# One row maximum over two score banks instead of two maxima

## The chip, the cores and the metric

The kernel runs on one core of a Trainium2 chip. The metric is the device time of one launch in microseconds (us); the time before is the median of three runs. One further execution was recorded by the hardware profiler, and all rows below come from it. Engines are named as in the profile: PE (matrix multiplications), PEld (its weight loads), DVE (vector engine), ACT (scalar engine), POOL (GpSimd), SP (the queue that issues DMAs). PSUM, where matmuls write, has eight banks of 512 fp32 numbers per partition.

## What is computed

An attention with a learned decay, and then a mixture of four experts on its output. Cut to what matters:

```python
# q, k, v: (4, 8, 576, 64); s: (4, 8, 576)
scores = scale * np.matmul(q, k.transpose(0, 1, 3, 2))
cum = np.cumsum(np.maximum(s, 0.0), axis=-1)
bias = -(cum[:, :, :, None] - cum[:, :, None, :])
scores = np.where(causal, -1000000000.0, scores + np.minimum(bias, 0.0))
scores = scores - np.max(scores, axis=-1, keepdims=True)
attn = np.exp(scores)
attn = attn / (np.sum(attn, axis=-1, keepdims=True) + 1e-09)
x = np.matmul(attn, v)        # then reshaped to (2304, 512)
for e in range(4):            # experts, 512 -> 1024 -> 512
    out += p[:, e:e + 1] * (np.maximum(x @ w1[e], 0.0) @ w2[e])
```

## The kernel before

There are 32 heads (`BH`). The 576 rows of a head are cut into five query tiles, m = 0 to 4; because of the causal mask tile m needs only its first 64, 192, 320, 448 or 576 scores. The list `VISITS` says which tiles of which head are done together: the first eight heads come twice (tiles 0 to 2, later tiles 3 and 4), the other 24 once with all five. So tile 4, the last, occurs 32 times.

For each tile the chain is: scores on PE into a bank `S` (line 584 for the first heads, one fp32 matmul; line 587 for the others, two matmuls for each piece), row maximum on DVE (line 597, a fused instruction that adds the mask, scales, writes the scores to SBUF tile `a` and keeps the maximum in `mx`, followed by a short instruction that reads the accumulator), exponential and row sum on ACT (line 605), 1/sum (lines 611, 613), the normalisation (line 402, mostly POOL), transposes on PE into a bank `T` (line 635), copies out of it by ACT (407) and DVE (671), and the product with v on PE into `pv` (694).

PSUM holds two `S` banks, two `T` banks, two for `pv` and two `mo` banks for the expert. Tile 4 has 576 scores and does not fit one bank, so it is made in two pieces of 288, each in one `S` bank: matmuls and a maximum for each piece, the second maximum starting from the first one's result:

```python
pieces = [(0, bb)] if bb <= 512 else [(0, 288), (288, bb)]
```

The order of all engines' instructions in this part is written out before the kernel is built, by a list scheduler (`Sched`). A task names its engines with an assumed cost, its priority, and the buffers that it takes and gives back. Each engine takes the ready task of the best priority whose buffers are free. `S` tiles may also borrow an `mo` bank (`sources`). While attention runs, PE's gaps are filled with matmuls of the first expert (lines 786 and 799) at a lower priority, and early on with matmuls that only keep PE busy (line 426). What is left of the first expert, and the other three (lines 1087, 1097), follow after the last attention task. PE takes its instructions strictly in the order that results, and so do the others. The waits between engines are put in when the program is built: an instruction waits on another engine's counter until the last accesses of a buffer that it reuses are done.

Of the kernel before, what the change touches and what calls it, by code (L numbers as in the profile page):

```python
# [139 lines left out]
class Task:  # L140
    def __init__(self, engs, fn, deps, prio, take, give, xfer):
        self.engs = {e: c if isinstance(c, tuple) else (c, 0) for e, c in engs.items()}
        self.fn, self.prio, self.take, self.give, self.xfer = fn, prio, take, give, xfer
        self.wait = 0
        self.ready = 0.0
        self.next = []
        self.after = []
        self.done = None
        self.eng = None
        self.act = 0.9  # L150
        self.port = ()
        self.both = False


class Sched:
# [30 lines left out]
        return t  # L186

    def sources(self, t, p, lend):
        if p in ("S", "T") and lend:
            return (p, "mo")  # L190
        if t.prio < 1000.0 * NH + 900:
            return LEND.get(p, (p,))
        return (p,)

    def run(self, until):
# [22 lines left out]
        while left:  # L218
            moved = False
            lend = not any(t.prio >= 1e6 and t.ready <= now + LAHEAD for t in cand["PE"])  # L220
            nxt = []
            for e in names:
                if free[e] > now:
                    nxt.append(free[e])
                    continue
                best = None
                for t in cand[e]:
                    if best is not None and t.key > best.key:
                        continue
                    if t.ready + t.engs[e][1] > now:  # L230
                        nxt.append(t.ready + t.engs[e][1])
                        continue
                    if t.xfer is not None and self.dma_free > now + BACKLOG:
                        nxt.append(self.dma_free - BACKLOG)
                        continue
                    if e in t.port and self.port > now:
                        nxt.append(self.port)
                        continue
                    ok = True
                    for p, k in t.take:  # L240
                        f = min((b[0] for x in self.sources(t, p, lend) for b in self.pools[x]), default=1e18)
                        if f > now:
                            ok = False
                            if f < 1e17:
                                nxt.append(f)
                            break
                    if ok:
                        best = t
                if best is None:
                    if e == "PE" and self.warm and active() < FILL:  # L250
                        x = dummy(now)
                        if x:
                            free[e] = now + x
                            nxt.append(free[e])
                            moved = True
                    elif e == "PE" and self.warm:
                        nxt.append(now + 100)
                    continue
                t = best
                extra = 0  # L260
                if e == "PE" and now > T_HAM:
                    self.warm = None
                if e == "PE" and self.warm and t.prio < 1e6 and active() < KEEP:
                    extra = dummy(now)
                moved = True
                for x in t.engs:
                    cand[x].remove(t)
                for p, k in t.take:
                    x, b = min(((x, b) for x in self.sources(t, p, lend) for b in self.pools[x]), key=lambda y: y[1][0])
                    self.pools[x] = [y for y in self.pools[x] if y is not b]  # L270
                    self.tok[p, k] = b[1]
                    self.home[p, k] = x
                t.fn(e)
                end = now + extra + t.engs[e][0]
                if e == "PE":
                    acts.append((now + extra, end, t.act))
                free[e] = end
                if e in t.port:
                    self.port = end
                if t.xfer is not None:  # L280
                    self.dma_free = max(self.dma_free, end + 700) + t.xfer / RATE
                    end = self.dma_free + 900
                t.done, t.eng = end, e
                left.discard(id(t))
                for p, k in t.give:
                    self.pools[self.home.pop((p, k))].append([end + 150, self.tok.pop((p, k))])
                for n in t.after:
                    n.wait -= 1
                    if n.wait == 0:
                        for x in n.engs:  # L290
                            cand[x].append(n)
                for n in t.next:
                    n.wait -= 1
                    n.ready = max(n.ready, end + (LAG[e][0] if e in n.engs else LAG[e][1]))
                    if n.wait == 0:
                        for x in n.engs:
                            cand[x].append(n)
                nxt.append(free[e])
            if not moved:
                later = [x for x in nxt if x > now]  # L300
                assert later, "schedule stuck"
                now = min(later)


def body(ctx, tc, qk, vp, s, dp, w1, w1s, w2, w2s, out):
# [10 lines left out]
    def make(name, n, shape, dt=F32, pool=apool):  # L316
        sch.pool(name, [pool.tile(shape, dt, name=f"{name}_{i}") for i in range(n)])
# [21 lines left out]
    def AB(j, dt=F32R):  # L339
        return slot(tok["AB", j], [P, 2, S], dt, apool)  # L340

    pattn = actx.enter_context(tc.tile_pool(name="psa", bufs=1, space=PSUM))
    make("S", 2, [P, 512], pool=pattn)
    make("T", 2, [P, 512], pool=pattn)
    make("pv", 1, [P, 1024], pool=pattn)
    make("mo", 2, [P, 512], pool=psum)
# [152 lines left out]
    for j, (h, ms) in enumerate(VISITS):  # L499
# [36 lines left out]
        else:  # L536
            if pq:
                qk_ready = [ld, ldc]
            else:
# [7 lines left out]
                def f(e, j=j, h=h, ext=ext):  # L547
                    nc.sync.dma_start(out=tok["KK", j][0:64, :, 0:ext].bitcast(F32), in_=AB(j)[64:128, 0:1, 0:ext].bitcast(F32).to_broadcast([64, 2, ext]))
                    nc.sync.dma_start(out=tok["KK", j][64:128, 0, 0:ext].bitcast(F32), in_=AB(j)[64:128, 1, 0:ext].bitcast(F32))
                    nc.sync.dma_start(out=tok["KK", j][64:68, 1, 0:ext].bitcast(F32), in_=ced[h, 2:6, 0:ext])  # L550
# [17 lines left out]
        for m in ms:  # L568
# [2 lines left out]
            n = bb - a  # L571
            c = (j, m)

            pieces = [(0, bb)] if bb <= 512 else [(0, 288), (288, bb)]
            prev = None
            for pi, (j0, j1) in enumerate(pieces):
                lastp = pi == len(pieces) - 1

                def f(e, j=j, a=a, j0=j0, j1=j1, c=c, pi=pi, ext=ext, pq=pq, h=h):
                    t = tok["S", (c, pi)]  # L580
                    if pq:
                        r = AB(j, F32)
                        w = min(P, ext - a)
                        nc.tensor.matmul(t[0:w, 0:j1 - j0], r[0:66, 0, a:a + w], r[0:66, 1, j0:j1], start=True, stop=True)  # L584
                    else:
                        for x, k in ((0, P), (1, 68)):
                            nc.tensor.matmul(t[:, 0:j1 - j0], AB(j)[0:k, x, a:a + P], tok["KK", j][0:k, x, j0:j1], start=(x == 0), stop=(x == 1))  # L587
                qt = sch.add({"PE": (t_pe4(j1 - j0) if pq else 2 * t_pe(j1 - j0))}, f, qk_ready + [last_q], prio=pr + pi, take=[("S", (c, pi))],
                             give=([("AB", j)] if pq else [("AB", j), ("KK", j)]) if lastp and m == ms[-1] else [])
                last_q = qt  # L590
                qt.act = 0.5 if pq else 0.9
                firstq.setdefault(j, qt)

                def f(e, m=m, n=n, a=a, j0=j0, j1=j1, c=c, pi=pi):
                    mx = tok["mx", c]
                    z = tok[f"a{m}", c]
                    nc.vector.tensor_tensor_reduce(  # L597
                        out=z[0:n, j0:j1], in0=tok["S", (c, pi)][0:n, 0:j1 - j0], in1=mask[0:n, 448 - a + j0:448 - a + j1], scale=-0.125,
                        scalar=1e30 if pi == 0 else mx[0:n, 0:1], op0=ALU.add, op1=ALU.min, accum_out=mx[0:n, pi:pi + 1])
                prev = sch.add({"DVE": t_dve(j1 - j0)}, f, [qt, prev], prio=pr + pi,  # L600
                               take=[("mx", c), (f"a{m}", c)] if pi == 0 else [], give=[("S", (c, pi))])

            def f(e, m=m, n=n, bb=bb, c=c, k=len(pieces) - 1):
                z = tok[f"a{m}", c]
# [685 lines left out]
```

## Time and profile before

| what | value |
|---|---|
| median of three runs | 942.4 us (941.18, 942.4, 942.45) |
| the profiled execution, its own time | 941.22 us |
| span of its instructions | 939.3 us |
| PE busy over the span | 926.9 us (99%) |
| DVE busy | 714.4 us (76%) |
| PE clock granted, mean | 0.999 of full speed |

The span runs from the first to the last instruction; 1.9 us of the execution's time lie around it. Attention with the first expert's matmuls between takes up about the first 300 us. A matmul counts as busy while it is in flight, and those in flight overlap, so PE can be shown busy while its next instruction waits a short time.

### The profile page before, as it was taken

To read this page: it belongs to the slowest core of one execution; us is meant where nothing else is said; L and a number is where in the kernel's file an instruction comes from. 1 tells how busy PE (TensorE), PEld (TensorE's weight loads), DVE (VectorE), ACT (ScalarE), POOL (GpSimd) and SP (SyncE) were. 2 spreads that over 40 slices of the span, in tenths; PEclk is the share of its full clock that TensorE was granted. 3 is DMA by queue.
4 is the path that set the end of the run, shared out by engine and by line. 5 is a ranking of instruction groups with operands and counts; after the bars stand their busy time and mean duration, and the time that the engine had idled before them with its cause. 6 is when DMAs were issued, how large, how long until landed. Compare 5 with 4: busy or idle time off the path is not lost.

```text
span 939.3 us, 18269 instructions
## 1 busy us (share of the span) xinstructions
PE 926.9 (99%) x6304; PEld 881.9 (94%) x6304; DVE 714.4 (76%) x1803; ACT 454.6 (48%) x1167; POOL 456.5 (49%) x504
## 2 busy tenths in 40 slices
PE   9999999999999999999999999999999999999998
PEld 7778998898998998999999999999999999999998
DVE  7898887888886221368679977988797879678976
ACT  6788796777875110252444333434252524343340
POOL 5566574555641789312653173435343714471222
PEclk9999999999999999999999999999999999999999
DMA  5887677687642895487765558654785458744613
GB/s 154 235 220 217 179 202 213 169 214 209 168 123 99 272 386 194 168 299 261 235 230 177 195 195 281 201 185 155 256 276 182 140 202 278 235 153 150 220 33 118
DMA packets 125899, 189.73 MB, mean 202 GB/s; under 512 B 10432, under 2 KB 102112, under 8 KB 125808
## 3 DMA queue, kind: packets, MB, share of 16 engines
q1 hardware_dynamic: 125808, 188.57, 63.6%
q8 instruction: 50, 0.82, 0.4%
q14 instruction: 41, 0.34, 0.1%
HBM read 144.73 MB, written 29.54 MB: 186 GB/s over the span
## 4 chain that ended last, share of the span: by engine, by line
PE 89%; DVE 4%; issue 2%; ACT 2%; POOL 1%; DMA 1%; DVEq 0%; SPq 0%; ACTq 0%; POOLq 0%
PE pb L1087 26%; PE pb L1097 20%; PE mo L1097 8%; PE mo L799 7%; PE mo L786 6%; PE T L635 5%; PE pv L694 5%; PE S L587 4%; PE pb L786 3%; PE pb L799 3%; PE S L584 2%; DVE aTl L671 1%; DVE a L597 1%; ACT a L605 1%; DMA AB_f<-cx 1%
## 5 line engine op out<-in xcount | busy, mean ns | idle before, releaser
L1087 PE MATMUL pb<-x,w1h 128*128 128x384 f32 x1008 | 256.7, 335 | 0.5 <-ACT t L1127 0.3
L1087 PEld LDWEIGHTS pb<-x,w1h 128*128 128x128 f32 x1008 | 180.8, 188 | 2.5 <-DVE t L1131 1.8
L1087 PE MATMUL pb<-x,w1l 128*128 128x384 f32 x504 | 168.5, 334 | 0.0
L394 POOL TENSOR_TENSOR hT_r<-t,hT_r 128x768 fp32r<-128x768 f32 x18 | 34.0, 1887 | 268.6 <-PE pb L1087 215.6
L1127 ACT ACTIVATE t<-pb 128x384 f32<-128x384 f32 x144 | 66.4, 486 | 160.8 <-PE pb L1087 151.6
L1190 DVE SCALAR_TENSOR_TENSOR acc<-pb,prob,acc 128x256 f32<-128x256 f32 x288 | 125.8, 473 | 5.3 <-PE pb L1097 4.9
L1097 PE MATMUL pb<-w2h,hT_r 128*128 128x256 f32 x720 | 114.6, 283 | 0.1
L402 POOL TENSOR_SCALAR a<-a,sm 128x192 f32<-128x192 f32 (+4 forms) x142 | 79.9, 569 | 50.2 <-DVE sm L613 36.4
L1097 PEld LDWEIGHTS pb<-w2h,hT_r 128*128 128x128 f32 x720 | 99.6, 191 | 0.3 <-issue 0.3
L605 ACT ACTIVATE a<-a,mx 64x64 f32<-64x64 f32 (+4 forms) x160 | 89.3, 561 | 21.5 <-DVE mx L597 18.8
L1131 DVE TENSOR_TENSOR t<-pb,t 128x384 f32<-128x384 f32 x108 | 54.4, 549 | 57.6 <-PE pb L1087 36.1
L1087 PEld LDWEIGHTS pb<-x,w1l 128*128 128x128 f32 x504 | 94.6, 188 | 0.0
L1104 ACT ACTIVATE hT_r<-t 128x768 fp32r<-128x768 f32 x54 | 45.7, 846 | 98.2 <-PE pb L1097 92.7
L1101 DVE SCALAR_TENSOR_TENSOR t<-t 128x768 f32<-128x768 f32 x72 | 88.0, 1223 | 1.7 <-issue 1.6
L786 PE MATMUL mo<-xg,w1h 128*128 128x256 f32 (+1 forms) x360 | 83.6, 309 | 0.9 <-DVE hT_r L792 0.9
L407 ACT ACTIVATE aTh<-T 128x64 fp32r<-128x64 f32 (+2 forms) x278 | 66.3, 307 | 22.3 <-PE T L635 19.3
L635 PE MATMUL T<-idn,a 128*128 128x128 f32 x465 | 73.1, 276 | 3.5 <-DVE aTl L671 3.2
L671 DVE TENSOR_TENSOR aTl<-T,aTh 128x64 fp32r<-128x64 f32 (+3 forms) x246 | 72.6, 334 | 4.5 <-ACT aTh L407 3.3
L1097 PE MATMUL pb<-w2l,hT_r 128*128 128x256 f32 x360 | 71.5, 283 | 0.0
L597 DVE CUSTOM_DVE_ANT_0 a<-S,mask 128x320 f32<-128x320 f32 (+4 forms) x151 | 61.7, 420 | 8.9 <-PE S L584 4.2
L635 PEld LDWEIGHTS T<-idn,a 128*128 128x128 f32 x465 | 53.2, 141 | 15.4 <-issue 6.5
L1190 DVE SCALAR_TENSOR_TENSOR acc<-mo,prob,acc 128x256 f32<-128x256 f32 x144 | 62.7, 472 | 1.6 <-PE mo L1097 1.6
(149 smaller groups left out, 2086.8 us busy)
## 6 DMA issues: line engine op xcount, KB each, us to landing
x<-xs_d SPq DMA_DIRECT2D x68, 768.0 KB
x<-x_d SPq DMA_DIRECT2D x55, 768.0 KB
xs_d<-x SPq DMA_DIRECT2D x12, 768.0 KB
raw<-in_qk_dram SPq DMA_DIRECT2D x24, 288.0 KB
KK<-AB_r SPq DMA_DIRECT2D x24, 288.0 KB
x_d<-xh SPq DMA_DIRECT2D x12, 576.0 KB
w1r<-in_w1s_dram SPq DMA_DIRECT2D x6, 1024.0 KB
w2r<-in_w2s_dram SPq DMA_DIRECT2D x6, 1024.0 KB
```

The costliest lines, as they stand in the source:

```text
L402: (nc.gpsimd if e == "POOL" else nc.vector).tensor_scalar(out, in_, scale, 1.0 if bias is None else bias, op0=ALU.mult, op1=ALU.mult if bi ...
L597: nc.vector.tensor_tensor_reduce(out=z[0:n, j0:j1], in0=tok["S", (c, pi)][0:n, 0:j1 - j0], in1=mask[0:n, 448 - a + j0:448 - a + j1], scale ...
L605: nc.scalar.activation(z[0:n, 0:bb], z[0:n, 0:bb], AF.Exp, bias=tok["mx", c][0:n, k:k + 1], scale=-1.0, accum_out=tok["sm", c][0:n])
L635: nc.tensor.transpose(t[:, 128 * k:128 * k + 128], z[:, 128 * x:128 * x + 128], idn)
L671: nc.vector.tensor_tensor(out=dst, in0=src, in1=h_.bitcast(F32), op=ALU.subtract)
L786: nc.tensor.matmul(t[:, 0:w], wl[q][:, dc, o:o + P], xgt[:, l, dc, 0:w], start=(u == 0), stop=(u == 3 * KD - 1))
L799: nc.tensor.matmul(t, ht[:, fc, 128 * ti:128 * ti + 128], wl[fc // 2][:, fc % 2, :], start=(u == 0), stop=(u == 3 * KF - 1))
L1087: nc.tensor.matmul(ts[u][:, 0:TG], wv[wl][:, k, 128 * u:128 * u + 128], x[:, xl_, k, :], start=start and k == 0 and n == 0, stop=k == 1 an ...
L1097: nc.tensor.matmul(ts[t][:, 0:256], h_part(o, hl_)[:, k, 128 * t:128 * t + 128], wv[wl][:, k, :], start=start and k == 0 and n == 0, stop= ...
L1101: (nc.gpsimd if e == "POOL" else nc.vector).scalar_tensor_tensor(out=out, in0=in0, scalar=0.0, in1=in1, op0=ALU.max, op1=op)
L1127: nc.scalar.activation(tmp[name][:, u], ts[u][:, 0:TG], f)
L1190: nc.vector.scalar_tensor_tensor(out=a_, in0=ts[t][:, 0:256], scalar=prob[:, tt, e:e + 1], in1=a_, op0=ALU.mult, op1=ALU.add)
```

## The change

The two `S` banks become one PSUM tile of 1024 columns, `both`, and the two pool entries are its halves. Tiles 0 to 3 take one half as before. Tile 4 takes both halves at once (`whole`): its four matmuls write columns 224 to 511 and 512 to 799, which are neighbours across the bank border, and one row-maximum instruction reads all 576. A task that is `whole` can start only when both halves are free, and it may not borrow an `mo` bank. The planner's cost of the maximum becomes that of 576 columns, and the four matmuls are one task.

```diff
     def sources(self, t, p, lend):
-        if p in ("S", "T") and lend:
+        if p in ("S", "T") and lend and not t.whole:
             return (p, "mo")
...
                         f = min((b[0] for x in self.sources(t, p, lend) for b in self.pools[x]), default=1e18)
+                        if t.whole and p == "S":
+                            f = max(b[0] for b in self.pools[p]) if len(self.pools[p]) == 2 else 1e18
...
-    make("S", 2, [P, 512], pool=pattn)
+    both = pattn.tile([P, 1024], F32, name="S")
+    sch.pool("S", [both[:, 0:512], both[:, 512:1024]])
...
-            pieces = [(0, bb)] if bb <= 512 else [(0, 288), (288, bb)]
+            pieces = [(0, bb)]
+            halves = [(0, bb)] if bb <= 512 else [(0, 288), (288, bb)]
...
-                    t = tok["S", (c, pi)]
+                    for j0, j1 in halves:
+                        t = (tok["S", (c, pi)] if len(halves) == 1 else both[:, 224:800])[:, j0:j1]
...
-                            nc.tensor.matmul(t[:, 0:j1 - j0], AB(j)[0:k, x, a:a + P], tok["KK", j][0:k, x, j0:j1], start=(x == 0), stop=(x == 1))
+                                nc.tensor.matmul(t, AB(j)[0:k, x, a:a + P], tok["KK", j][0:k, x, j0:j1], start=(x == 0), stop=(x == 1))
-                qt = sch.add({"PE": (t_pe4(j1 - j0) if pq else 2 * t_pe(j1 - j0))}, f, qk_ready + [last_q], prio=pr + pi, take=[("S", (c, pi))],
+                whole = len(halves) > 1
+                held_s = [("S", (c, x)) for x in range(len(halves))]
+                qt = sch.add({"PE": sum(t_pe4(y - x) if pq else 2 * t_pe(y - x) for x, y in halves)}, f, qk_ready + [last_q], prio=pr + pi, take=held_s,
...
+                    t = both[:, 224:800] if whole else tok["S", (c, pi)]
...
-                        out=z[0:n, j0:j1], in0=tok["S", (c, pi)][0:n, 0:j1 - j0], in1=mask[0:n, 448 - a + j0:448 - a + j1], scale=-0.125,
+                        out=z[0:n, j0:j1], in0=t[0:n, 0:j1 - j0], in1=mask[0:n, 448 - a + j0:448 - a + j1], scale=-0.125,
...
-                               take=[("mx", c), (f"a{m}", c)] if pi == 0 else [], give=[("S", (c, pi))])
+                               take=[("mx", c), (f"a{m}", c)] if pi == 0 else [], give=held_s)
```

Since the scheduler plans anew, the order of the whole attention part shifts. On PE, this is one head's scores in the kernel before (`S_0` and `S_1` are the two banks, `KK` and `AB` the head's keys and queries; 320 is tile 2, 448 tile 3, the two of 288 tile 4; DVE_49 is DVE's counter):

```order
L587 MATMUL S_1_98<-KK_0_110,AB0_r_815 128x320 [waits DVE_49]
L587 MATMUL S_1_98<-KK_0_110,AB0_r_815 128x320
L587 MATMUL S_0_97<-KK_0_110,AB0_r_815 128x448 [waits DVE_49]
L587 MATMUL S_0_97<-KK_0_110,AB0_r_815 128x448
L799 MATMUL mo_1_103<-w2h3_88,hT0_r_596 128x512 [waits Activation_49]
L799 MATMUL mo_1_103<-w2h0_85,hT1_r_604 128x512
L587 MATMUL S_1_98<-KK_0_110,AB0_r_815 128x288 [waits DVE_49]
L587 MATMUL S_1_98<-KK_0_110,AB0_r_815 128x288
```

Each tile has its own wait for the maximum that frees its bank. This is the same place of the same head's scores in the changed kernel (line 593 is what was line 587, 809 what was 799, `S_97` the one tile):

```order
L593 MATMUL S_97<-KK_0_109,AB0_r_876 128x320 [waits DVE_49]
L593 MATMUL S_97<-KK_0_109,AB0_r_876 128x320
L593 MATMUL S_97<-KK_0_109,AB0_r_876 128x448 x2
L809 MATMUL mo_0_101<-w2l0_89,hT0_r_593 128x512
L809 MATMUL mo_0_101<-w2l1_90,hT0_r_593 128x512 x2
L809 MATMUL mo_0_101<-w2l2_91,hT0_r_593 128x512
```

The 448 columns of tile 3 go to the other half than the 320 of tile 2 and have no wait of their own any more: the wait in front of the 320 covers both halves. Tile 4 comes a product with v (line 704, before 694) and five transposes later, all four matmuls behind one wait:

```order
L645 MATMUL T_0_98<-idn_74,a4_1_127 128x128 [waits Pool_49]
L645 MATMUL T_0_98<-idn_74,a4_1_127 128x128
L645 MATMUL T_1_99<-idn_74,a4_1_127 128x128 x3
L593 MATMUL S_97<-KK_0_109,AB0_r_876 128x288 [waits DVE_49]
L593 MATMUL S_97<-KK_0_109,AB0_r_876 128x288 x3
```

The scores of tile 4, which stood in two parts at two places, now stand in one block.

## Rows read from the trace of the kernel before

**Rows 1.** The page: span, and PE's busy time, share and instructions.
```profile
span 939.3 us, 18269 instructions
PE 926.9 (99%) x6304; PEld 881.9 (94%) x6304; DVE 714.4 (76%) x1803; ACT 454.6 (48%) x1167; POOL 456.5 (49%) x504
```

**Rows 2.** Busy time of each engine in four stretches; columns in the first line.
```profile
core 0: us, PE busy (x) PEld busy (x) DVE busy (x) ACT busy (x) POOL busy (x), PEclk, DMA share, GB/s
0.00:40.00 40.00, 37.88 (x214) 29.14 (x215) 30.55 (x156) 28.04 (x108) 23.42 (x50) 1.00 0.70 192
40.00:300.00 260.00, 255.30 (x1739) 230.07 (x1738) 218.20 (x864) 204.26 (x674) 145.09 (x288) 1.00 0.66 184
300.00:420.00 120.00, 118.84 (x698) 109.78 (x698) 40.19 (x68) 28.70 (x61) 71.56 (x48) 1.00 0.74 257
420.00:940.00 520.00, 514.88 (x3660) 512.96 (x3658) 425.44 (x718) 193.65 (x325) 216.42 (x119) 1.00 0.60 199
```

**Rows 3.** The chain that ended last, from 40 to 300 us: shares by line.
```profile
by line: PE mo L799 17.3%; PE T L635 15.6%; PE pv L694 14.5%; PE mo L786 13.6%; PE S L587 13.0%; issue 5.7%; DVE aTl L671 4.0%; PE S L584 2.5%; DVE a L597 2.2%; ACT a L605 2.1%; ACT aTh L407 1.2%; DVE xr L709 1.2%; ACT xr L704 1.1%; DVE V L
```

**Rows 4.** Groups by line and shape, 40 to 300 us: count, busy us, mean ns, idle before.
```profile
L605 ACT ACTIVATE a<-a,mx 128x576 f32<-128x576 f32 x30 | 23.3, 777 | 10.2 <-DVE mx L597 8.9 <-DVE sm L613 0.7
...
L597 DVE CUSTOM_DVE_ANT_0 a<-S,mask 128x448 f32<-128x448 f32 x30 | 18.3, 609 | 1.4 <-PE T L635 1.1 <-PE S L587 0.4
...
L597 DVE CUSTOM_DVE_ANT_0 a<-S,mask,mx 128x288 f32<-128x288 f32 x30 | 15.3, 509 | 2.8 <-PE S L587 1.4
...
L597 DVE CUSTOM_DVE_ANT_0 a<-S,mask 128x288 f32<-128x288 f32 x30 | 13.3, 442 | 0.0
...
L597 DVE CUSTOM_DVE_ANT_0 a<-S,mask 128x320 f32<-128x320 f32 x24 | 11.5, 478 | 1.6 <-PE S L587 1.5
...
L597 DVE DVE_READ_ACCUMULATOR2_ANT mx<- 128x1 f32 x138 | 11.0, 80 | 0.0
...
L597 DVE CUSTOM_DVE_ANT_0 a<-S,mask 128x192 f32<-128x192 f32 x24 | 8.3, 345 | 0.6 <-PE S L587 0.5
```

**Rows 5.** Who waited for whom, 40 to 300 us: total us, times, longest.
```profile
DVE a L597 <- PE S L587: 3.8, 8, 0.9
...
PEld S L587 <- DVE mx L597: 3.4, 10, 0.5
...
PE S L587 <- DVE mx L597: 0.7, 3, 0.3
```

**Rows 6.** Timeline around tiles 1 to 4 of one head: start us, duration us, instruction.
```profile
204.39 0.33 DVE L597 CUSTOM_DVE_ANT_0 a<-S,mask 128x192 f32<-128x192 f32 x1
204.65 0.08 DVE L597 DVE_READ_ACCUMULATOR2_ANT mx<- 128x1 f32 x1
204.65 0.48 DVE L597 CUSTOM_DVE_ANT_0 a<-S,mask 128x320 f32<-128x320 f32 x1
204.78 0.30 PEld L587 LDWEIGHTS S<-KK,AB_r 128*128 128x128 f32 x2 [0.23 <-DVE mx L597]
204.82 0.64 PE L587 MATMUL S<-KK,AB_r 128*128 128x448 f32 x2
...
205.06 0.07 DVE L597 DVE_READ_ACCUMULATOR2_ANT mx<- 128x1 f32 x1
...
205.50 0.51 PE L587 MATMUL S<-KK,AB_r 128*128 128x288 f32 x2
...
205.66 0.60 DVE L597 CUSTOM_DVE_ANT_0 a<-S,mask 128x448 f32<-128x448 f32 x1
...
206.20 0.07 DVE L597 DVE_READ_ACCUMULATOR2_ANT mx<- 128x1 f32 x1
...
206.42 0.44 PE L587 MATMUL S<-KK,AB_r 128*128 128x288 f32 x2
```

**Rows 7.** The chain's longest pieces: start us, duration us, work (early filling matmuls).
```profile
3.90 3.13 PE mo L426 x17
```

More of the change, by code (lines that the diff above doesn't have):

```diff
@@ L152, in __init__ @@
         self.both = False
+        self.whole = False
 class Sched:
@@ L577, in body @@
                 lastp = pi == len(pieces) - 1
-                def f(e, j=j, a=a, j0=j0, j1=j1, c=c, pi=pi, ext=ext, pq=pq, h=h):
-                    t = tok["S", (c, pi)]
[L581 to L586, printed above, removed]
-                            nc.tensor.matmul(t[:, 0:j1 - j0], AB(j)[0:k, x, a:a + P], tok["KK", j][0:k, x, j0:j1], start=(x == 0), stop=(x == 1))
@@ L588, in body, with f @@
-                qt = sch.add({"PE": (t_pe4(j1 - j0) if pq else 2 * t_pe(j1 - j0))}, f, qk_ready + [last_q], prio=pr + pi, take=[("S", (c, pi))],
+                def f(e, j=j, a=a, halves=halves, c=c, pi=pi, ext=ext, pq=pq, h=h):
+                    for j0, j1 in halves:
+                        t = (tok["S", (c, pi)] if len(halves) == 1 else both[:, 224:800])[:, j0:j1]
+                        if pq:
+                            r = AB(j, F32)
+                            w = min(P, ext - a)
+                            nc.tensor.matmul(t[0:w], r[0:66, 0, a:a + w], r[0:66, 1, j0:j1], start=True, stop=True)
+                        else:
+                            for x, k in ((0, P), (1, 68)):
+                                nc.tensor.matmul(t, AB(j)[0:k, x, a:a + P], tok["KK", j][0:k, x, j0:j1], start=(x == 0), stop=(x == 1))
@@ L589, in body, with f @@
+                whole = len(halves) > 1
+                held_s = [("S", (c, x)) for x in range(len(halves))]
+                qt = sch.add({"PE": sum(t_pe4(y - x) if pq else 2 * t_pe(y - x) for x, y in halves)}, f, qk_ready + [last_q], prio=pr + pi, take=held_s,
                              give=([("AB", j)] if pq else [("AB", j), ("KK", j)]) if lastp and m == ms[-1] else [])
                 last_q = qt
+                qt.whole = whole
                 qt.act = 0.5 if pq else 0.9
                 firstq.setdefault(j, qt)
-                def f(e, m=m, n=n, a=a, j0=j0, j1=j1, c=c, pi=pi):
+                def f(e, m=m, n=n, a=a, j0=j0, j1=j1, c=c, pi=pi, whole=whole):
```

## The prediction

> **What bounds the kernel now.** I read the page first. PE is busy for 926.9 of 939.3 us [rows 1], so time is lost or won only where PE's instructions come later or earlier; the change removes no work from PE. Next I cut the span into stretches [rows 2]. The change touches attention alone, which ends near 300 us; behind it DVE is busy for a third of its time (40.2 of 120 us) and then for 425 of 520 us beside a PE that never stands, and nothing there is edited. From 40 to 300 us PE is busy for 255.3 of 260 us and DVE for 218.2, or 84%. So DVE is the second fullest engine, but not a full one. The 4.7 us that PE shows as idle are too few, because a matmul in flight counts as busy. The chain that ended last says the same from the other side [rows 3]: from 40 to 300 us some 76% of it are PE's own lines (17.3 + 15.6 + 14.5 + 13.6 + 13.0 + 2.5), while DVE's named lines have 7.4% (4.0 + 2.2 + 1.2), which is 19 us. The scores themselves (L587 and L584) make up 15.5% of it: they are on the path.
>
> Then I looked at how PE and DVE pass the two score banks back and forth. In the timeline of one head [rows 6] the 192-column maximum is over at 204.73 (204.65 + 0.08), and the 448-column scores, which go into the bank that it frees, start at 204.82, their weight load having waited for just that. So PE takes a score bank as soon as DVE lets go of it. And while PE writes there, from 204.82 to 205.46, DVE reads the 320 columns in the other bank, from 204.65 to 205.13. This overlap is what two separate banks give.
>
> **The change, part by part.** *The maxima.* There are 32 tiles with 576 scores. Each cost DVE 442 + 509 + 2 x 80 = 1111 ns [rows 4]. No row has 576 columns. From 320 (478 ns) to 448 (609 ns) a column costs 131/128 = 1.02 ns, so 576 come to 609 + 128 x 1.02 = 740 ns, with one accumulator read 820 ns. I take that, since the four lengths measured lie close to one line. At most the one instruction costs as much as the two, 951 ns, and only the second accumulator read is saved (80 ns); at least it costs no more than the 448 columns, 689 ns with its read (422 ns saved). DVE gets 32 x 0.291 = 9.3 us back, bounds 2.6 and 13.5.
>
> What of that reaches the path? DVE's work from 40 to 300 us shrinks by 9.3/218.2 = 4.3%; of the 19 us that DVE's lines have on the chain this is 0.8 us. Directly, L597 has 2.2% of 260 us, 5.7 us, on the chain; tile 4 has 28.6 of the 66.7 us of L597's instructions (43%, 2.5 us), and these get 26% shorter: 0.6 us. I take the sum, -1.4 us; bounds 0 and -9.3 us.
>
> The notes known as the Trainium skill, "Perfetto Trace Analysis", section "Optimizing Scalar/DVE Operations", say that grouping DVE operations helps if the engine is saturated, and that breaking them up may help if it is not saturated but leaves gaps on other engines. By its about 125 ns of overhead for each PSUM operation the grouping would be worth an estimated 32 x 0.125 = 4.0 us of DVE time, against the 9.3 us from the rows, which hold the accumulator read too. At 84% the trace puts this kernel on the side of breaking up, which speaks against the change.
>
> *The waits of the other tiles.* The two halves now belong to one PSUM tile, and the built program treats them as one: the write into a half waits for the last maximum that stands before it in the program, of either half. The order shows it: the wait ahead of the 320 columns covers the 448 in the other half, where each had its own. I went through the program's wait values: at 35 places a tile of 64 to 448 columns waits for a maximum of the other half, which no place did before. What is waited for is 17 times a read of 192 columns, 9 times of 320, 5 times of 448, 4 times of 64. By [rows 4], each with its accumulator read (the 64 counted as 192, so an upper end), that is 21 x 0.425 + 9 x 0.558 + 5 x 0.689 = 17.4 us. This is the most: PE gets there the moment its own half is free and stands through the whole other read. The least is 0: PE comes late enough. The example [rows 6] is near the upper end: with such a wait the 448 columns would start not at 204.82 but after the 320's accumulator read ends at 205.13, at 205.22, 0.40 us of the 0.56 later. But the view of waits [rows 5] has only 4.1 us in 13 waits for this pair, the short ones being hidden in flight, so not every place is like this. I take half: 8.7 us of standing PE. What queues behind it on PE is everything: transposes, products with v and the expert's filling matmuls. DVE likewise waits at 53 of its maxima for scores of the other half; since DVE is the one that lags, as the 0.09 us between release and write show, I count this at nothing. Had it no lag, each could cost a pair of matmuls, 0.64 us for the longest [rows 6], 53 x 0.64 = 34 us, on an engine with 42 us to spare.
>
> *Tile 4 itself.* Its first piece used to go when the first bank was free: at 205.50, before DVE had even begun the 448 columns at 205.66 [rows 6]. Now all four matmuls wait for that read as well, until 206.27. The old second piece started at 206.42 and had this wait anyway. So what is lost is work that PE could do ahead of that wait and now can't: the first piece, at most 0.44 us, as long as the two matmuls from 206.42 take with their flight [rows 6], 32 times 14.1 us. The planner knows of this wait and puts products and transposes ahead of it, as the order shows, so I take a quarter, 3.5 us; the least is 0. The tile's maximum is ready no earlier for being one instruction, since its scores all come before it.
>
> *The rest.* Early on the plan has 24 in place of 21 matmuls that only keep PE busy. At 3.13/17 = 0.18 us each [rows 7] that is 0 (where PE would stand) to 0.6 us; I take 0.3. Before the last attention task stand 17 fewer matmuls of the expert; they follow behind it, and PE's sum stays as it was.
>
> *The sum.* PE stands 8.7 + 3.5 = 12.2 us more. Part comes back, because while PE stands the other engines catch up and later waits shrink; PE's 76% of the chain says most does not. I count 60%, 7.3 us. From the profiled execution's 941.2: -1.4 + 7.3 + 0.3 gives 947.4 us. That execution lies 1.2 us under the median of the three runs, so the median should come out between 947.4 and 948.6; I say **948 us**, 0.6% slower.
>
> **The rivals.** *DVE's relief reaches PE, and it gets faster.* For it: ACT's exponential of the 576 columns stood 8.9 us for DVE's maximum [rows 4], and score writes follow releases within 0.1 us, so DVE hands the pace on. Against it: DVE has 16% idle and a small share of the chain. If half of the 9.3 us arrived and the planner had covered the new waits, the time would be 942.4 - 4.6 = about 938 us. It decides from the point where under a tenth of the 17.4 + 14.1 = 31.5 us of possible new waits stays on PE.
>
> *Nothing measurable.* PE finds its filling work between the score writes, the new waits are not exposed beyond a few us and meet DVE's 1.4 to 3: 941 to 944 us. For it: the shown waits for maxima are 4.1 us in all. Against it: the 0.09 us.
>
> *Lock step.* Every new wait is exposed, and PE's share of the chain passes on 76%: 0.76 x 31.5 = 24 us, less 1.4: about 942.4 + 22.5 = 965 us. For it: PE was at the release in the example. Against it: the planner put other work ahead of many writes.
>
> *The one instruction reads across the bank border at a price.* At the bound of 951 ns DVE saves 2.6 instead of 9.3 us; that moves my sum by 1 us, and changes no sign.
>
> **How the numbers follow.** I call a difference of up to 0.2%, 1.9 us, no change, about what a measurement of this kernel can tell. The forecast, 945 to 957 us, has a chance of 0.60; lock step beyond that 0.06; nothing measurable 0.17; faster 0.17. So slower 0.66, the same 0.17, faster 0.17. The range leaves out the worst lock step and the best half of the faster case: 938 to 957 us. The forecast's own range is 945 to 957.
>
> **What the changed profile would show.** Right: one maximum of 576 columns x32 at about 740 ns; DVE's busy time in attention some 9 us less; the waits of the scores' matmuls and weight loads for DVE's maxima well above 4.1 us; the first stretch of long expert matmuls without attention between them starting some 5 us later in time although fewer filling matmuls stand ahead. Wrong: score writes that start while the other half is being read as often as before, or waits that grow while the end of attention does not move. I would be wrong above all if PE came to the score writes later than the example shows, or if DVE's lag, which sets the release of score banks, were the real pace.

## The result and the profile after

The changed kernel takes 950.95 us (median of four runs, 949.49 to 951.3) against 942.42 us for the kernel before beside it (four runs, 941.18 to 943.24). The ratio is 1.0086, with a 95% interval of 1.0074 to 1.0099: slower by 0.86%, which is 8.1 us (the medians differ by 8.5). The forecast was 948, slower.

The top of the page of the changed kernel, for [rows 1]:

```profile
span 949.2 us, 18193 instructions
...
PE 933.0 (98%) x6307; PEld 883.1 (93%) x6307; DVE 710.8 (75%) x1742; ACT 456.3 (48%) x1164; POOL 452.1 (48%) x504
```

The span is 9.9 us longer. DVE has 61 instructions fewer and less work (710.8 against 714.4 us), so it is not DVE's sum that made the kernel longer. The stretches of [rows 2], in the changed kernel:

```profile
0.00:40.00 40.00, 37.11 (x204) 27.47 (x204) 28.93 (x147) 26.48 (x104) 20.88 (x49) 1.00 0.69 184
40.00:300.00 260.00, 251.36 (x1683) 223.25 (x1681) 211.27 (x798) 203.94 (x666) 143.18 (x289) 0.99 0.65 181
300.00:420.00 120.00, 120.00 (x714) 110.10 (x713) 36.99 (x69) 27.25 (x63) 71.60 (x48) 1.00 0.68 235
```

From 40 to 300 us PE got through 1683 matmuls where it did 1739: attention falls behind there. Where it ends is best read from the last product with v. The first row is line 694 of the kernel before, the last one line 704 of the changed kernel; the two times in it are the first and the last start:

```profile
L694 PE MATMUL pv<-aTl,V x176: 222/308/368, 43.2 to 298.6; 128*128 128x320 f32 x72, 128*128 128x256 f32 x48, 128*128 128x192 f32 x32, 128*128 128x128 f32 x24
```

```profile
L704 PE MATMUL pv<-aTl,V x176: 222/308/368, 45.0 to 307.2; 128*128 128x320 f32 x72, 128*128 128x256 f32 x48, 128*128 128x192 f32 x32, 128*128 128x128 f32 x24
```

Attention ends 8.6 us later (307.2 against 298.6), although 17 of the expert's matmuls fewer stand ahead of it. So most of the 9.9 us arises in attention.

The groups of [rows 4], 40 to 300 us, in the changed kernel:

```profile
L607 DVE CUSTOM_DVE_ANT_0 a<-S,mask 128x576 f32<-128x576 f32 x31 | 23.1, 746 | 3.1 <-PE S L593 1.7 <-PE T L645 1.3
...
L607 DVE CUSTOM_DVE_ANT_0 a<-S,mask 128x320 f32<-128x320 f32 x22 | 10.6, 482 | 6.1 <-PE S L593 6.0
...
L607 DVE DVE_READ_ACCUMULATOR2_ANT mx<- 128x1 f32 x109 | 8.7, 80 | 0.0
```

One maximum over 576 columns takes 746 ns. Two took 442 + 509 ns and a second accumulator read of 80 ns, so by these durations each tile gives DVE 285 ns back. But the 320 columns of tile 2 now find DVE waiting 6.0 us for their scores, where that was 1.5. The waits of [rows 5] show the same on both sides:

```profile
DVE a L607 <- PE S L593: 12.9, 23, 1.3
...
PEld S L593 <- DVE mx L607: 8.5, 17, 1.6
...
PE S L593 <- DVE mx L607: 3.7, 7, 1.2
```

Scores waiting for maxima: 12.2 us (8.5 + 3.7, as the forecast added them) instead of 4.1. Maxima waiting for scores: 12.9 instead of 3.8. Each engine now stands longer for the other.

One such place, in the timeline of the changed kernel (start us, duration us, instruction, and in brackets the idle time before it and what ended that):

```profile
170.33 0.74 DVE L607 CUSTOM_DVE_ANT_0 a<-S,mask 128x576 f32<-128x576 f32 x1
...
170.99 0.08 DVE L607 DVE_READ_ACCUMULATOR2_ANT mx<- 128x1 f32 x1
...
171.13 0.68 PE L593 MATMUL S<-KK,AB_r 128*128 128x448 f32 x2 [1.10 <-DVE mx L607]
...
171.84 0.62 DVE L607 CUSTOM_DVE_ANT_0 a<-S,mask 128x448 f32<-128x448 f32 x1
...
172.39 0.08 DVE L607 DVE_READ_ACCUMULATOR2_ANT mx<- 128x1 f32 x1
...
172.53 0.41 PE L593 MATMUL S<-KK,AB_r 128*128 128x64 f32 x2 [0.39 <-DVE mx L607]
```

The maximum over 576 columns releases both halves at 171.07. The 448 columns of tile 3 take one; the 64 columns of another head's tile 0 go to the other half, which is free from 171.07 on. They start at 172.53 all the same, just behind the accumulator read of the 448: the program's wait asks for DVE's 451st count where the half itself would need the 446th. In the kernel before, DVE read one bank while PE wrote the other [rows 6].

### The profile page after: what moved, and what is told of

Its sections match the earlier page's. It is cut to its first block, busy times and chain, and to the rows that moved or that the text cites. A ratio compares the mean times of both kernels' runs of the same rounds, so it can differ in the third digit from the quotient of the medians.

```text
span 949.2 us, 18193 instructions
## 1 busy us (share of the span) xinstructions
PE 933.0 (98%) x6307; PEld 883.1 (93%) x6307; DVE 710.8 (75%) x1742; ACT 456.3 (48%) x1164; POOL 452.1 (48%) x504
## 4 chain that ended last, share of the span: by engine, by line
PE 80%; DVE 4%; issue 2%; DMA 2%; ACT 2%; POOL 1%; SPq 0%; DVEq 0%; POOLq 0%; ACTq 0%
PE pb L1097 26%; PE pb L1107 20%; PE mo L1107 8%; PE mo L809 6%; PE mo L796 4%; PE pb L796 3%; PE S L593 3%; PE T L645 3%; PE pv L704 3%; PE pb L809 3%; DVE aTl L681 1%; DVE a L607 1%; ACT aTh L411 0%; ACT a L615 0%; DMA AB_r<-ce_d 0%
## 5 line engine op out<-in xcount | busy, mean ns | idle before, releaser
L607 DVE CUSTOM_DVE_ANT_0 a<-S,mask 128x576 f32<-128x576 f32 (+4 forms) x149 | 71.0, 488 | 22.9 <-PE S L593 12.9
L796 PE MATMUL mo<-xg,w1h 128*128 128x256 f32 (+1 forms) x352 | 79.5, 309 | 0.0
L645 PE MATMUL T<-idn,a 128*128 128x128 f32 x462 | 75.3, 277 | 2.6 <-DVE aTl L681 1.4
L411 ACT ACTIVATE aTh<-T 128x256 fp32r<-128x256 f32 (+4 forms) x277 | 67.9, 306 | 20.5 <-PE T L645 16.9
L681 DVE TENSOR_TENSOR aTl<-T,aTh 128x256 fp32r<-128x256 f32 (+3 forms) x245 | 72.4, 336 | 6.6 <-ACT aTh L411 5.5
```

The lines of the kernel that those rows point to most:

```text
L411: nc.scalar.activation(out, in_, AF.Copy)
L607: nc.vector.tensor_tensor_reduce(out=z[0:n, j0:j1], in0=t[0:n, 0:j1 - j0], in1=mask[0:n, 448 - a + j0:448 - a + j1], scale=-0.125, scalar= ...
L645: nc.tensor.transpose(t[:, 128 * k:128 * k + 128], z[:, 128 * x:128 * x + 128], idn)
L681: nc.vector.tensor_tensor(out=dst, in0=src, in1=h_.bitcast(F32), op=ALU.subtract)
L796: nc.tensor.matmul(t[:, 0:w], wl[q][:, dc, o:o + P], xgt[:, l, dc, 0:w], start=(u == 0), stop=(u == 3 * KD - 1))
```

## The experiments

Twelve kernels ran. Differences below are the ratio to the kernel before, less one, times 942 us; that puts the changed kernel at +8.1.

**Shared waits alone.** The kernel before, with its two banks made halves of one tile. Every engine has the order of the kernel before; by the program's wait values 73 score writes and 104 maxima now wait for work on the other half as well.

```diff
-    make("S", 2, [P, 512], pool=pattn)
+    both = pattn.tile([P, 1024], F32, name="S")
+    sch.pool("S", [both[:, 0:512], both[:, 512:1024]])
```

> The kernel before with one edit: the two score banks are halves of one PSUM tile. Pieces, maxima and the order on every engine stay word for word; only the waits change: the program has 73 score writes and 104 maxima that wait for an access to the other half, where before has none. Theory of shared waits (the forecast's main term): PE stands as the forecast says, slower by 6 to 12 us, 948 to 955 us. Rival theory, that the new order and tile 4's need for both halves cost the time: no change, 941 to 944 us. The score writes' waits for maxima, 4.1 us in the view of waits of before, should grow to over 10 us by the first and stay by the second.

Measured: 960.08 us against 942.1, ratio 1.0191 (1.0177 to 1.0205), +18.0 us. The waits from 40 to 300 us in this kernel:

```profile
PEld S L588 <- DVE mx L598: 22.4, 47, 1.1
...
DVE a L598 <- PE S L588: 14.8, 26, 1.3
PE S L588 <- DVE mx L598: 7.3, 21, 0.8
```

These were 3.4, 3.8 and 0.7 us [rows 5]. No instruction was added, removed or moved, so the shared tile costs time by its waits alone, and more of it than I had expected: DVE's waits grew along with PE's.

**One maximum without the shared waits.** The changed kernel with the same instructions in the same order. For every pair of accesses to different halves the dependence is taken out, and each access depends on the last one of the other engine to its own bank.

```diff
+        for old, of, was in seen:
+            if of != engine and not at & was:
+                tc.declare_no_dep(inst.ins, old.ins, reason="other score bank")
+        for x in at:
+            last = next((old for old, of, was in reversed(seen) if of != engine and x in was), None)
...
+                tc.add_manual_dep(inst.ins, last.ins.name, mybir.DependencyInfo(mybir.DependencyClass.Sync, mybir.DependencyReason.DATA), reason="own score bank")
```

> The changed kernel word for word, one tile and one maximum of 576, but the waits between accesses that touch different halves are left out (accesses to a half still wait for the last ones to the same half, so nothing is unordered that shares a bank). 126 score writes wait for their own half, 9 for more. Theory of shared waits: 941 to 946 us, and 1 to 2 us below the two-tile version of the same order, which is what the shorter maximum is worth. Theory that DVE's relief is worth most of its 9.3 us: 934 to 939 us, faster than before. Theory of the order: 949 to 952 us.

Measured: 943.12 us, ratio 1.0013 (1.0004 to 1.0022), +1.2 us. The same waits in this kernel:

```profile
DVE a L625 <- PE S L611: 5.6, 11, 1.2
...
PEld S L611 <- DVE mx L625: 3.4, 5, 1.5
...
PE S L611 <- DVE mx L625: 2.0, 2, 1.2
```

So 6.9 of the changed kernel's 8.1 us go with the shared waits, DVE's waits as much as PE's. What is left is just above the kernel before, though each of 32 maxima costs DVE 285 ns less, 9.1 us in all.

**The new order with two banks and two maxima.** The changed kernel's order on PE, ACT, POOL and SP, but two tiles and tile 4's maximum in two.

```diff
-    both = pattn.tile([P, 1024], F32, name="S")
-    sch.pool("S", [both[:, 0:512], both[:, 512:1024]])
+    make("S", 2, [P, 512], pool=pattn)
...
+                    for x0, (j0, j1) in enumerate(halves):
...
+                            out=z[0:n, j0:j1], in0=tok["S", (c, x0)][0:n, 0:j1 - j0], in1=mask[0:n, 448 - a + j0:448 - a + j1], scale=-0.125,
```

> The changed kernel's order on PE, ACT, POOL and the DMA queue, tile 4 taking both banks at once, but the banks are two PSUM tiles again and each half of tile 4 has its own maximum. So: the new plan without the shared waits and without the shorter maximum. Theory of shared waits: most of the loss goes, 942 to 946 us. Rival theory (order and both banks at once): as slow as the changed kernel or slower by the lost relief, 949 to 954 us.

Measured: 949.88 us, ratio 1.0087 (1.0073 to 1.0101), +8.2 us. My own number was missed; the rival's came. With neither the shared waits nor the single maximum, the new plan alone, in which tile 4 takes and returns both banks together, costs what the whole change costs. Two things in it are not the order of PE. The plan also chooses between engines: of the subtractions that DVE and POOL share (line 394 of the kernel before) it gives DVE 135 instead of 130. And tile 4's two maxima stand back to back on DVE at all 32 tiles, where the kernel before has other work between them at 23. One such pair in the trace of this kernel:

```profile
207.55 0.45 DVE L606 CUSTOM_DVE_ANT_0 a<-S,mask 128x288 f32<-128x288 f32 x1
207.92 0.08 DVE L606 DVE_READ_ACCUMULATOR2_ANT mx<- 128x1 f32 x1
208.15 0.52 DVE L606 CUSTOM_DVE_ANT_0 a<-S,mask,mx 128x288 f32<-128x288 f32 x1
208.59 0.08 DVE L606 DVE_READ_ACCUMULATOR2_ANT mx<- 128x1 f32 x1
```

The second maximum reads the first one's `mx` and starts 0.15 us after its accumulator read. From the first start to the last accumulator read, where the next instruction can start, such a pair holds DVE for 1030 ns (mean of the 32), one maximum of 576 columns for 673 (170.33 to 170.99 in the timeline above). So in this order one maximum frees 0.36 us a tile, 11.4 us in all, more than the durations say.

**Shared waits and two maxima.** The changed kernel with only the maximum split, out of the one tile.

```diff
+                    for x0, (j0, j1) in enumerate(halves):
...
+                            out=z[0:n, j0:j1], in0=(both[:, 224:800] if len(halves) > 1 else tok["S", (c, 0)])[0:n, j0:j1], in1=mask[0:n, 448 - a + j0:448 - a + j1], scale=-0.125,
```

> The changed kernel with its one tile, its order and its shared waits, but tile 4's maximum split in two again (288 and 288 columns), which gives the 9.3 us back to DVE. Sum of the forecast: 1.4 us slower than the changed kernel, 951 to 954 us. Theory that the relief is worth most of its 9.3 us: 957 to 961 us.

Measured: 959.12 us, ratio 1.019 (1.0175 to 1.0204), +17.9 us. This closes a square of four kernels whose order on PE, ACT, POOL and SP is one and the same:

| | two maxima | one maximum | one instead of two |
|---|---|---|---|
| own waits for each half | +8.2 | +1.2 | -7.0 |
| shared waits | +17.9 | +8.1 | -9.8 |
| price of sharing | +9.7 | +6.9 | |

One maximum instead of two is worth 7 to 10 us here, far above the 1.4 of the forecast. By the intervals, each of these differences is uncertain by some 1.5 to 2 us.

The granted clock has a share in them. Its mean over an execution was 0.9997 in the kernel before, 0.9985 and 0.9965 in the two kernels with own waits (two maxima, one), and 0.9944 and 0.9988 in the two with shared waits. Within the executions of one kernel, 0.001 less clock went with about 0.5 us more time (145 executions in 16 sets, each held against the mean of its own set; an estimate). At the clock of the kernel before the square would read about +7.6 and -0.4 with own waits, +15.2 and +7.6 with shared ones. One maximum is then worth about 8 us in both rows, and sharing costs about 8 us in both columns.

**DVE's relief alone.** The kernel before in its own order, where tile 4's second maximum reads only 4 of its 288 columns. It leaves the other scores of that piece out of the result; their place in `a` is set to zero once at the start.

```diff
+                    w_ = j1 - j0 if pi == 0 else 4
...
-                        out=z[0:n, j0:j1], in0=tok["S", (c, pi)][0:n, 0:j1 - j0], in1=mask[0:n, 448 - a + j0:448 - a + j1], scale=-0.125,
+                        out=z[0:n, j0:j0 + w_], in0=tok["S", (c, pi)][0:n, 0:w_], in1=mask[0:n, 448 - a + j0:448 - a + j0 + w_], scale=-0.125,
```

> The kernel before, its order word for word and its two score tiles, but tile 4's second maximum reads only 4 of its 288 columns (the other columns' scores are left out of the result). By the price of a column this takes about 0.29 us from each of the 32 tiles, 9.3 us of DVE time, as the one instruction of the change does, with nothing else moved. The forecast's term: 1.4 us faster, 940 to 942 us. Theory from the last four runs, that the relief is worth 7 to 8 us wherever it is given: 934 to 936 us.

Measured: 937.62 us against 941.68, ratio 0.996 (0.9948 to 0.9972), -3.8 us. Neither number came; it lies between them. The short maximum in the groups of this kernel:

```profile
L598 DVE CUSTOM_DVE_ANT_0 a<-S,mask,mx 128x4 f32<-128x4 f32 x31 | 6.6, 214 | 2.8 <-PE S L587 1.4
```

It takes 214 instead of 509 ns, 295 ns less, close to the 285 of the change. So 9.4 us of DVE (32 x 0.295) bring 3.8 us, 40%, without any new order.

**Tile 4's scores into whichever half is free.** As the kernel without shared waits, but the scores of tile 4 are two tasks, and the first need not wait until both halves are free.

```diff
-                        if t.whole and p == "S":
-                            f = max(b[0] for b in self.pools[p]) if len(self.pools[p]) == 2 else 1e18
...
+            for x0 in range(len(halves)):
...
+                        y = 0 if own is half[0] else 1
...
+                        t = both[:, 224 + j0:224 + j1]
...
+                qt = sch.add({"PE": t_pe4(w1_) if pq else 2 * t_pe(w1_)}, f, qk_ready + [last_q], prio=pr + x0, take=held_s[x0:x0 + 1],
```

> As the version without shared waits (one maximum of 576 columns), but tile 4's scores are two tasks again: the first takes whichever half is free, writes the 288 columns that belong there, and the second takes the other half later. So tile 4 no longer has to find both halves free at once. Theory that the need for both halves at once made the new order 8 us dearer: 934 to 938 us, faster than before. Theory that the order lost its 8 us to something else: 941 to 945 us.

Measured: 945.12 us, ratio 1.004 (1.0027 to 1.0053), +3.8 us. That is at the upper end of the second theory: it does not get the order's price back. Its plan is a new one, though, and moves 18 of POOL's 504 instructions to DVE and ACT, so not only the halves differ.

**A half kept for tile 4.** As the kernel without shared waits, but while a tile 4 is ready and waits, no later task may take a score half.

```diff
+                    kept = not t.whole and any(u.whole and u.key < t.key and u.ready <= now for u in cand["PE"])
...
+                        f = min((b[0] for x in self.sources(t, p, lend) if not (kept and x == "S") for b in self.pools[x]), default=1e18)
```

> As the version without shared waits, tile 4 taking both halves at once, but while such a task is ready and waits, no task of a later priority may take a score half (it may borrow an expert bank). Theory that tile 4 loses by later tiles taking the halves ahead of it: 937 to 941 us. Theory that holding both halves at once is itself the price: 942 to 946 us.

Measured: 945.55 us, ratio 1.0033 (1.0021 to 1.0045), +3.1 us. Nor does this; the number of the second theory came.

**Either half, two maxima.** The plan of the kernel with either half first, with tile 4's maximum split in two.

```diff
+                for x0, (j0, j1) in enumerate(halves):
+                    t = both[:, 224 + j0:224 + j1] if whole else tok["S", (c, 0)][:, 0:bb]
...
+                        scalar=1e30 if x0 == 0 else mx[0:n, 1:2], op0=ALU.add, op1=ALU.min, accum_out=mx[0:n, k:k + 1]), "DVE", half[x0] if whole else tok["S", (c, 0)])
```

> The plan of the version in which either half goes first, its waits by bank, but two maxima of 288 columns instead of one of 576. Against that version it shows once more what the one maximum is worth: 1 to 2 us by the forecast, 7 to 8 us by the last four runs. If the plan is as good as the one of before, this one should come out near before, 941 to 945 us.

Measured: 948.15 us, ratio 1.0071 (1.0059 to 1.0083), +6.7 us. Against its sister with one maximum that is +2.9 us: in this order the relief is worth 3, between the two numbers named, and the plan is not as good as the one of before.

**How far plans scatter.** The last four ask what a mere new plan does. Two are the kernel before with another assumed cost for tile 4's maxima: 350 instead of 370 for each piece, and 522 and 590 ns, which are the traced durations with their accumulator reads (442 + 80, 509 + 80, rounded up). Two are the kernel without shared waits, planned with 820 and with 740 instead of 670 for its one maximum.

```diff
-                prev = sch.add({"DVE": t_dve(j1 - j0)}, f, [qt, prev], prio=pr + pi,
+                prev = sch.add({"DVE": t_dve(j1 - j0) if len(pieces) == 1 else (522, 590)[pi]}, f, [qt, prev], prio=pr + pi,
```

Plan with 350:

> The kernel before, two tiles and two maxima, with only the planner's assumed cost of each of tile 4's two maxima changed from 370 to 350 ns: same instructions, another order. It tells what a new plan by itself does. Theory that the changed order's 8 us come from the way tile 4 holds both halves: within 2 us of before, 940 to 944 us. Theory that any new plan of this kernel costs that much, the order of before being a lucky one: 945 to 950 us.

Plan with 522 and 590:

> As the last, with the assumed costs set to what the trace shows, 522 and 590 ns. Theory of holding both halves: within 3 us of before, 939 to 945 us. Theory of the lucky order: 945 to 950 us.

One maximum, plan with 820:

> The version without shared waits, one maximum, tile 4 taking both halves at once, planned again with an assumed cost of 820 ns for that maximum (what the trace shows) instead of 670. Theory of holding both halves: 941 to 946 us as with 670. If new plans differ by several us by themselves, this one differs from 943 us by 3 us or more to either side, and may beat before by up to 4 us.

One maximum, plan with 740:

> The same with 740 ns, the sum that the planner assumed for the two maxima before. Same expectations: 941 to 946 us by the theory of holding both halves, further from 943 us if plans differ by themselves.

Measured, against 942.97 us: 942.1 with 350, ratio 0.9991 (0.9978 to 1.0003); 936.53 with 522 and 590, ratio 0.9931 (0.9909 to 0.9952); 947.76 with 820, ratio 1.0045 (1.0028 to 1.0063); 945.6 with 740, ratio 1.0023 (1.0008 to 1.0038). In microseconds: -0.8, -6.5, +4.2, +2.2. The kernel with the traced costs, for which neither theory left room, beats both kernels though only two assumed costs were edited. Its attention, by the last product with v, and its stretch from 40 to 300 us:

```profile
L694 PE MATMUL pv<-aTl,V x176: 222/308/368, 43.4 to 291.5; 128*128 128x320 f32 x72, 128*128 128x256 f32 x48, 128*128 128x192 f32 x32, 128*128 128x128 f32 x24
```

```profile
40.00:300.00 260.00, 257.85 (x1768) 233.37 (x1767) 209.77 (x859) 207.29 (x681) 154.01 (x294) 1.00 0.67 188
```

Attention ends at 291.5 instead of 298.6 us, and PE does 1768 matmuls in the stretch instead of 1739. The top of its page shows what else the plan did:

```profile
PE 925.8 (99%) x6305; PEld 881.4 (94%) x6305; DVE 703.9 (75%) x1795; ACT 454.9 (49%) x1168; POOL 463.6 (50%) x511
```

DVE is busy for 10.5 us less than in the kernel before [rows 1] and POOL for 7.1 us more: with dearer maxima the planner gives DVE 118 of the shared subtractions instead of 130. So this kernel has a relief of DVE too, by another way. How much of the 6.5 us comes from it, and how much from the order, no run separates. Truer costs do not help as such: the 820 that fits the one maximum best (746 + 80 ns) gave +4.2 us where 670 gave +1.2, and put 138 of the subtractions on DVE.

## Why the prediction came out right, and which terms were wrong

The sign and the mechanism were right. The sum was short by 1.9 us by the ratio. That it came so near is in part luck: two of its three terms were missed by 5.6 and 5.8 us, in opposite directions.

- **The other tiles' shared waits, +5.2 (60% of 8.7).** The mechanism is shown: the waits alone cost 18.0 us in the old order, taking them out of the changed kernel brings 6.9 back, and adding them to two maxima costs 9.7. The term is too small by 1.7 us, and two things in the rows can account for it. DVE's waits for scores of the other half were counted as nothing, because DVE lags; but they grew from 3.8 to 12.9 us, and fall to 5.6 without the shared waits (no run separates their price from that of PE's waits). And in this order nothing is seen of the part that "comes back": the 12.2 us in which scores wait for maxima fall to 5.4 without sharing, 6.8 us, and the time falls by 6.9. In the old order part does come back: there these waits grow by 25.6 us (4.1 to 29.7) and the time by 18.0, 70%.
- **DVE's relief, -1.4.** The price of the instruction was right: 740 ns forecast, 746 measured, and no extra price for the bank border that a row would show. What failed is the step from DVE's time to the path. I took the shares of DVE's lines on the chain as the measure of what a shorter maximum can bring. It brings 3 to 10 us, by the order that it is in: 2.9, 3.8, 7.0 and 9.8 in four comparisons, about 4 to 8 at like clocks, by the estimate above. An order planned for one short maximum, in which two fit badly, can be part of the 7.0; but the kernel with either half first was planned for one as well, and there it is 2.9. The 3.8 in the old order have no such excuse and are already 2.7 times the term. A maximum that ends earlier also frees the score bank and starts the exponential earlier, and so may pull in PE's work, which the chain books under PE's lines; that this is the way is my reading, and no run shows it by itself.
- **Tile 4 itself and the order, +2.1 (60% of 3.5) and +0.3.** The new plan alone, with both banks taken and returned together, costs 8.2 us with two maxima, so the term was too small by some 6 us. With one maximum and own waits the same plan costs only 1.2. How much of this is tile 4's waiting for both halves is open. Letting it take either half first, or keeping one for it, gave +3.8 and +3.1 us against +1.2. As far as two new plans can show it, that speaks against the forecast's picture of a first piece held up. By assumed costs alone three plans of the kernel before differ by 6.5 us and three of the kernel without shared waits by 3.0, so much of the 8 us can be a poor plan as well as the block of four matmuls. Against mere chance stands that all five orders with one maximum and no shared waits lie at +1.2 to +4.2, though each has DVE's relief in it. What stays open is which cause common to the five makes up the difference. It can be that both halves come back at the end of one long maximum, or that DVE has 131 to 138 of the shared subtractions in them, against 130 in the kernel before and 118 in the fastest one.
- **The sum.** In the order in which the runs allow it: the new order +8.2, one maximum -7.0, shared waits +6.9, together +8.1. The forecast had +2.4, -1.4 and +5.2.
- **Two readings.** PE stands for 4.4 us of its last stretch (514.9 us busy of 519.3 up to the end of the span [rows 1, rows 2]), where the forecast says never. And the 66.7 us of line 597 leave out its 64-column maxima, 4.9 us from 40 to 300 us; with them tile 4 has 40% instead of 43%. Neither moves a term.

Of the rivals, relief that reaches PE was half right: it arrives, and with the order left alone a like relief made the kernel 3.8 us faster, but the plan and the waits took it back. Lock step, at +22.5 us, did not come in the changed kernel; the old order with shared waits comes near it with +18.0. There the two halves alternate more: of its 73 score writes that wait for the other half 52 belong to tiles 0 to 3, and counted alike the changed kernel has 37 (the forecast's 35 leave out two whose wait was already met). A price at the bank border of more than a few ns is excluded by the 746 ns. The signs named for a right forecast came: attention's end moved by 8.6 us where some 5 were named, and DVE's busy time from 40 to 300 us fell by 6.9 where some 9 were, part of it because some attention had by then moved out of that stretch. Over the whole span it fell by 3.6 us only: in one and the same order one maximum takes 6.4 us from it (717.1 to 710.7 us with own waits), and the plan's five more subtractions are on the other side. Of the two things that would have proved the forecast wrong above all, the second came in part: DVE's lag does set the pace in places, or its relief would not be worth 3 us and more.

The rule of the Trainium skill, "Perfetto Trace Analysis", section "Optimizing Scalar/DVE Operations", by which grouping can pay if the engine is saturated, did not separate the cases here: with DVE 82 to 84% busy from 40 to 300 us, one instruction instead of two was worth 2.9, 7.0 and 9.8 us in the three comparisons made. What made the kernel slower was not the larger instruction but what else it came with: a shared tile and another plan.

## What to carry to other kernels

Two buffers that are filled and drained in turn should stay two for the dependence tracking too: joining them so that one instruction can read both made accesses to one half wait for the other, at 7 to 18 us here. The share of an engine's lines on the chain is not what a shorter instruction can bring where it frees a buffer for the busiest engine: the 1.4 us from it were too low in all four comparisons, with gains of 2.9 to 9.8 us for some 9 us of instruction time. And where a planner orders the work and shares it out among engines, first ask how far its plans scatter (here 6.5 and 3.0 us by assumed costs alone), since a price of that size can be the plan's.

## What the hardware showed unexpectedly

The granted clock of PE fell in the changed kernel after PE had stood. Windows of that trace; columns as in [rows 2]:

```profile
160.00:165.00 5.00, 3.65 (x27) 2.89 (x26) 3.44 (x12) 4.41 (x13) 1.79 (x3) 1.00 0.80 243
...
170.00:172.00 2.00, 0.90 (x6) 0.69 (x5) 1.92 (x11) 1.47 (x7) 1.30 (x4) 1.00 0.88 289
172.00:174.00 2.00, 1.61 (x13) 1.47 (x12) 1.43 (x10) 1.50 (x8) 1.31 (x5) 0.89 0.85 210
174.00:176.00 2.00, 2.00 (x10) 1.86 (x9) 1.51 (x7) 1.97 (x10) 1.55 (x5) 0.50 0.41 92
176.00:178.00 2.00, 2.00 (x11) 1.70 (x9) 1.04 (x5) 1.39 (x5) 0.94 (x2) 0.76 0.00 0
```

PE was busy for 3.65 of 5 and for 0.90 of 2 us, and then had 0.50 of its clock from 174 to 176 us, the lower of the two levels (1.2 GHz), while it was full again. The kernel before stays at 1.00 throughout that stretch, though PE is busy there for 1.29 of 2 us from 172 and for 1.53 of 2 us from 174 us. So new waits can cost twice, as they did here, as standing time and as slower work behind it. In the changed kernel it is the smaller part: two executions of the changed kernel with a mean clock of 1.000 took 950.67 and 949.49 us, two with 0.997 and 0.998 took 951.23 and 951.3, about 1.2 us more.

One DVE instruction that reads across the border of two PSUM banks pays nothing visible for it: 746 ns for 576 columns, against 740 from the line through 320 and 448 columns [rows 4]. The Trainium skill bears on it: "Advanced Engine Details and Errata", section "The Read-Write Bubble", names one instruction reading several PSUM banks as possible on this chip, and the trace agrees with the 746 ns.
